# Attention features feeding a gated MLP on one core: the first batch alone, four MLP blocks instead of five beside the attention, the key sums on VectorE, gates after both halves

## The chip, the cores and the metric

The kernel runs on one core of a Trainium2 chip. The metric is the device time of one execution in microseconds; the median of three runs of the kernel before is 1408.88 us (1406.63 to 1411.75). TensorE (PE) multiplies matrices, VectorE (DVE), ScalarE (ACT) and GpSimd (POOL) work element by element, and SyncE (SP) issues all of the kernel's DMAs from one queue. Every engine takes its own instructions in the order in which they stand.

## The reference

```python
B, H, S, D, F = 8, 8, 576, 64, 128          # attention; the MLP is 4608 x 512 -> 1536 -> 512
def phi(x):
    proj = x @ w_phi                          # 64 -> 128
    proj = proj - max(abs(proj), axis=-1)
    return concat([exp(proj), exp(-proj)])    # 256 features
q_p, k_p = phi(q), phi(k)
kv = k_p.T @ v                                # per batch and head
z = sum(k_p, axis=tokens)
attn = (q_p @ kv) / (q_p @ z + 1e-6)
x = attn.reshape(4608, 512)
gate = 1 / (1 + exp(-(x @ w_gate)))
out = (gate * (x @ w_val)) @ w_out
```

All in float32. The MLP's weights come as float64 and are split on the chip into two float32r parts, `wh` and `wl`; x and the gated product are split alike (`xh`, `xl` and `hh`, `hl`), and each product of the MLP is three matmuls: high by high, and twice high by low.

## The kernel before

**Attention.** The 64 heads are 32 steps of two heads (a pair), four steps to a batch. A step projects the keys (`keys`, `rest`: tiles `pk`) and the queries (`q_half`: `pq`), takes the maximum of the keys on DVE, subtracts it (`dk`) and has ACT make the exponentials `ek` (`k_exp`); `q_max` does the maximum of the queries across partitions with a transposing reduction, small copies (line 506 has four of them) and a transpose, and subtracts it (`d`); `q_exp` makes `eq`. `kv` multiplies the key features by v into `kvz`, whose last third is the normalizer z; `turn` transposes it, `num` makes numerators `nm` and denominators `dp`; `norm` sends the denominators through two small DMAs (`dn`, `den`), takes the reciprocal, reads it back broadcast (`rb`) and multiplies (`xp`). x of batch 0 goes straight into `xh` and `xl` of the MLP's chunks 0 and 1; all of x goes to DRAM (`xscr`).

**MLP.** The hidden layer has 12 blocks of 128 (`j`). The first `JA` = 5 blocks run beside the attention (stage one), in 18 chunks of 256 tokens: a unit is one block of one chunk, two halves of 12 matmuls of 256 columns (gate, then value) into the two halves of one PSUM tile `gv`. The output of a chunk is two `acc` groups of three matmuls of 512 columns per block, stored to DRAM as y. After that, `rest_chunks` runs the other 7 blocks (stage two) in 9 chunks of 512 tokens, with matmuls of 512 columns (`g`, `v`, `acc2`), adds the stored y and writes the output. The weights of stage one are prepared by `weigh` between the first steps, three tiles to a block; those of stage two by `load_weights`, whose first pool takes the place of the attention's buffers, so that it runs while stage one ends.

**What sets the order.** In stage one the order on every engine is that of the program. A step has four places, each a call of `fill`: it adds to `due` and takes the halves and outputs whose turn has come from the list `ready`. Everything that follows a matmul (gate work, exponentials, sums, norm) is a generator in `tasks`: each `tick` advances all of them by one `yield`. `queue` puts the chunks of a finished batch in line `LAG` places later, `TILES` says how many weight tiles are granted by which step. Chunks that have no x yet are loaded by `load_x`.

In `half` the gate half is followed at once by ScalarE's two functions, which read the half that is done while the value half is still to be written to the same tile:

```python
            mm_in(gv[:, m, :], xs[c], js[i], m, CH)
            if m == 0:
                ...
                act.activation(t, gv[:, 0, :], AF.Tanh, scale=0.5)
                act.activation(u, gv[:, 0, :], AF.Exp)
            else:
                start(gate(c, i, n))
```

The normalizer's sum over the four 128-token tiles of keys is made by POOL (`k_sum`, lines 457 to 461) from step 4 on (`EARLY`); the steps before multiply each tile by ones on PE.

Of the kernel before, what the change touches and what calls it, by code (L numbers as in the profile page):

```python
# [33 lines left out]
JA = 5  # L34
JR = 8
EARLY = 4
DIRECT = 2
RATE = 3.0
LAG = (7, 9)
TILES = (1, 3, 5, 8, 11, 15)  # L40
# [4 lines left out]
def attention_moe(  # L45
# [154 lines left out]
    def half_units(js, mp, ps_gv, ps_acc):  # L200
        xs, hs, gvs, cs = {}, {}, {}, set()

        def load_x(c):
            xh, xl, raw = x_tiles(mp, CH, f"1_{c}")
            xs[c] = xh, xl
            nc.sync.dma_start(raw, xscr[c])
            for _ in range(3):
                yield
            act.copy(xh, raw)
            yield  # L210
            vec.tensor_tensor(xl, raw, xh.bitcast(F32), op=ALU.subtract)  # L211

# [4 lines left out]
        def gate(c, i, n):  # L217
            gv = gvs.pop((c, i))
            u, t, hh, hl = hs[c, i]
# [6 lines left out]
            vec.tensor_tensor(hl, u, hh.bitcast(F32), op=ALU.subtract)  # L226

        def half(c, i, m):
            if c not in xs:
                begin(c)  # L230
                for _ in range(4):
                    tick()
# [3 lines left out]
            gv = gvs[c, i]  # L236
            mm_in(gv[:, m, :], xs[c], js[i], m, CH)
            if m == 0:
                u = mp.tile([P, CH], F32, tag="u", name="u" + n)
                t = mp.tile([P, CH], F32, tag="t", name="t" + n)  # L240
                hh = mp.tile([P, CH], F32R, tag="hh", name="hh" + n, bufs=7)
                hl = mp.tile([P, CH], F32R, tag="hl", name="hl" + n, bufs=7)
                hs[c, i] = u, t, hh, hl
                act.activation(t, gv[:, 0, :], AF.Tanh, scale=0.5)  # L244
                act.activation(u, gv[:, 0, :], AF.Exp)  # L245
            else:
                start(gate(c, i, n))
                if i >= 1:
                    begin(c + 1)

        def half_out(c, t):
            acc = ps_acc.tile([P, DM], F32, tag="acc", name=f"acc1_{c}_{t}")
            for i, j in enumerate(js):
                mm_out(acc, t, (*hs[c, i][2:], None), j, i == 0, i == len(js) - 1)
            y = mp.tile([P, DM], F32, tag="y", name=f"y1_{c}_{t}")
            act.activation(y, acc, AF.Copy, scale=0.5)  # L256
            nc.sync.dma_start(yscr[c][t], y)

        def chunk(c):
# [3 lines left out]
            for i in range(len(js)):  # L263
                for m in range(2):
                    items.append((1.45, lambda i=i, m=m: half(c, i, m)))
                if i < 2 and c:
                    items += outs(c - 1)[i : i + 1]
            return items

# [3 lines left out]
        return chunk, outs, xs  # L273
# [60 lines left out]
    with ExitStack() as actx:  # L334
# [74 lines left out]
        def k_exp(i, gs, pps, ns):  # L409
# [14 lines left out]
            if i < DIRECT:  # L424
                for g, pp, mx, e in zip(gs, pps, mxs, es):
                    mn = at.tile([P, 4], F32, tag=f"mn{g}", name=f"mn{i}_{g}")
                    vec.tensor_scalar(mn[:, :ns], mx[:, :ns], -1.0, None, op0=ALU.mult)
                    for t in range(ns):
                        for sg in (1, 0):
                            act.activation(  # L430
                                e[:, t, sg * F : sg * F + F], pp[:, t, :], AF.Exp,
                                bias=(mn, mx)[sg][:, t : t + 1], scale=1.0 - 2.0 * sg,
                            )
                return
# [17 lines left out]
        def k_sum(i):  # L452

            es = ks[i]
            su = at.tile([P, 2, 2 * F], F32, tag="su", name=f"su{i}")
            for hd in range(2):
                pool.tensor_tensor(su[:, hd, :], es[hd][:, 0, :], es[hd][:, 1, :], op=ALU.add)  # L457
                for t in (2, 3):
                    pool.tensor_tensor(su[:, hd, :], su[:, hd, :], es[hd][:, t, :], op=ALU.add)
            for hd in range(2):  # L460
                pool.tensor_tensor(
                    su[head(hd), hd, :], su[head(hd), hd, :], es[2][head(hd), 0, :],
                    op=ALU.add,
                )
            es.append(su)
# [9 lines left out]
        def rest(i):  # L475
# [4 lines left out]
            def go():  # L480
                yield from k_exp(i, (2,), [pp], 1)
                if i >= EARLY:
                    yield
                    k_sum(i)
# [31 lines left out]
        def kv(i):  # L516
# [13 lines left out]
            for t in range(4, 5) if su else range(5):  # L530
                for o in range(0, P, Q):
                    hd, sg = divmod(o // Q, 2)
                    fs = slice(sg * F, sg * F + F)
                    if su:
                        a, x = ones, su[0][:, hd, fs]
                    else:
                        a = ones if t < 4 else halves[:, hd, :]
                        x = (e0, e1)[hd][:, t, fs] if t < 4 else e2[:, 0, fs]
                    nc.tensor.matmul(
                        kvz[o : o + Q, 2 * F :], a, x,  # L540
                        start=t == 0 or bool(su), stop=t == 4, tile_position=(0, o),
# [53 lines left out]
        def norm(i, ex, dr):  # L595
            b, p = steps[i]
            dn = at.tile([P, 9], F32, tag="dn", name=f"dn{i}")
            rb = at.tile([P, S], F32, tag="rb", name=f"rb{i}", bufs=1)
            nc.sync.dma_start(dn, dr.rearrange("(o r) c -> o r c", r=Q)[:, 0, :])
# [3 lines left out]
            vec.reciprocal(dn, dn)  # L603
            nc.sync.dma_start(dens[i].rearrange("h (r c) -> (h r) c", c=9), dn)
# [5 lines left out]
            for _ in range(4):  # L610
# [3 lines left out]
            for c in range(S // CH if b == 0 else 0):  # L614
# [4 lines left out]
                split(xs[c][0][:, ps], xs[c][1][:, ps], xp[:, c * CH : c * CH + CH])  # L619
            t = 0  # L620
# [169 lines left out]
```

## Time and profile before

| | us |
|---|---|
| median of 3 runs | 1408.88 |
| profiled execution, its own time | 1405.74 |
| its span, first to last instruction | 1403.8 |
| busy: PE / PE weight loads | 1253.2 / 984.3 |
| busy: DVE / ACT / POOL | 787.9 / 538.4 / 175.3 |
| mean granted clock of TensorE, share of full | 0.961 |

The busy time of PE counts matmuls that overlap as one stretch; it says when PE had something in hand, not that it ran at its peak. An engine's idle time is put down to what ended it last. The granted clock is the share of TensorE's full 2.4 GHz that it was given; 0.5 is 1.2 GHz.

### The profile page before, as it was taken

How to read it: one execution, taken by the hardware profiler on the slowest of the kernel's cores; microseconds unless marked ns; L12 is line 12 of the kernel's file. 1: busy time of each engine (PE TensorE's matmuls, PEld its weight loads, DVE VectorE, ACT ScalarE, POOL GpSimd, SP SyncE). 2: the span in 40 equal slices, each digit the busy share in tenths (PEclk: the TensorE clock that was granted, in tenths of full speed). 3: DMA queues.
4: the chain of work that ended last, by engine and by line, in shares of the span. 5: the costliest groups of instructions: out<-in, count | busy, mean ns of one | idle time of the engine just before them, and what ended most of it. 6: DMA issues, size and time to landing. Idle time of an engine off the chain costs nothing.

```text
span 1403.8 us, 22704 instructions
## 1 busy us (share of the span) xinstructions
PE 1253.2 (89%) x9096; PEld 984.3 (70%) x9096; DVE 787.9 (56%) x1527; ACT 538.4 (38%) x1133; POOL 175.3 (12%) x230
## 2 busy tenths in 40 slices
PE   6666897887987999989888788999999999999998
PEld 3433666665765777766666777888888888888887
DVE  6878877654754777766546833773424434244233
ACT  5543554544453555554453332331212222222121
POOL 0022332312221331323110000000000000000000
PEclk9867899998998999999999999999999999999999
DMA  5666333232232233232216510641201202112010
GB/s 198 206 220 203 104 105 99 81 96 90 62 98 82 63 117 104 84 119 76 71 60 196 188 38 16 215 139 37 91 30 61 83 8 91 30 60 90 0 61 30
DMA packets 81737, 133.42 MB, mean 95 GB/s; under 512 B 18656, under 2 KB 38240, under 8 KB 81632
## 3 DMA queue, kind: packets, MB, share of 16 engines
q1 hardware_dynamic: 81632, 131.98, 29.3%
q8 instruction: 71, 1.16, 0.3%
q14 instruction: 34, 0.28, 0.1%
HBM read 93.91 MB, written 28.46 MB: 87 GB/s over the span
## 4 chain that ended last, share of the span: by engine, by line
PE 73%; DVE 10%; ACT 9%; DMA 5%; issue 2%; SPq 1%; DVEq 0%; ACTq 0%
PE acc L171 21%; PE gv L164 15%; PE g L164 12%; PE v L164 12%; PE kvz L524 4%; PE nm L575 3%; ACT ek L447 2%; PE dp L584 2%; ACT t L244 2%; DMA rb<-den 1%; PE pk L403 1%; ACT u L245 1%; ACT eq L561 1%; PE pq L393 1%; DMA den<-dn 1%
## 5 line engine op out<-in xcount | busy, mean ns | idle before, releaser
L164 PE MATMUL gv<-xh,wh 128*128 128x256 f32 x720 | 222.5, 309 | 84.4 <-ACT u L245 66.9
L164 PEld LDWEIGHTS gv<-xh,wh 128*128 128x128 f32 x720 | 141.9, 197 | 115.5 <-ACT u L245 84.2
L164 PE MATMUL gv<-xl,wh 128*128 128x256 f32 x720 | 208.9, 290 | 2.0 <-DVE xl L211 2.0
L164 PE MATMUL gv<-xh,wl 128*128 128x256 f32 x720 | 208.2, 289 | 0.0
L171 PE MATMUL acc<-wh,hh 128*128 128x512 f32 x432 | 172.9, 400 | 0.7 <-ACT y L256 0.7
L171 PE MATMUL acc<-wl,hh 128*128 128x512 f32 x432 | 170.0, 393 | 0.0
L171 PE MATMUL acc<-wh,hl 128*128 128x512 f32 x432 | 169.1, 391 | 0.0
L164 PEld LDWEIGHTS gv<-xl,wh 128*128 128x128 f32 x720 | 142.6, 198 | 3.4 <-DVE xl L211 2.9
L164 PEld LDWEIGHTS gv<-xh,wl 128*128 128x128 f32 x720 | 142.5, 198 | 0.0
L62 ACT CAST hh<-u 128x512 fp32r<-128x512 f32 x63 | 39.1, 621 | 201.1 <-DVE u L185 201.1
L224 ACT CAST hh<-u 128x256 fp32r<-128x256 f32 x90 | 36.5, 406 | 197.8 <-DVE u L223 197.6
L457 POOL TENSOR_TENSOR su<-ek 128x256 f32<-128x256 f32 x56 | 45.1, 806 | 510.0 <-issue 298.2
L183 DVE TENSOR_SCALAR t<-t 128x512 uint32<-128x512 uint32 x63 | 26.8, 426 | 138.6 <-ACT t L180 138.4
L524 PE MATMUL kvz<-ek,v 128*32 128x256 f32 x1280 | 87.7, 426 | 15.9 <-issue 8.7
L164 PE MATMUL g<-xh,wh 128*128 128x512 f32 x252 | 99.0, 393 | 0.0
L171 PEld LDWEIGHTS acc<-wh,hh 128*128 128x128 f32 x432 | 81.9, 190 | 24.1 <-issue 6.3
L164 PE MATMUL v<-xh,wh 128*128 128x512 f32 x252 | 98.6, 391 | 0.0
L164 PE MATMUL g<-xh,wl 128*128 128x512 f32 x252 | 98.5, 391 | 0.0
L164 PE MATMUL g<-xl,wh 128*128 128x512 f32 x252 | 98.5, 391 | 0.0
L164 PE MATMUL v<-xl,wh 128*128 128x512 f32 x252 | 98.4, 390 | 0.0
L164 PE MATMUL v<-xh,wl 128*128 128x512 f32 x252 | 98.2, 390 | 0.0
L180 ACT ACTIVATE t<-g 128x512 f32<-128x512 f32 x63 | 37.6, 597 | 150.8 <-PE g L164 150.7
(94 smaller groups left out, 2305.4 us busy)
## 6 DMA issues: line engine op xcount, KB each, us to landing
wraw<-w_moe SPq DMA_DIRECT2D x36, 512.0 KB
xl<-xs SPq DMA_DIRECT2D x34, 512.0 KB
k<-k SPq DMA_DIRECT2D x32, 320.0 KB
v<-v SPq DMA_DIRECT2D x32, 320.0 KB
q<-q SPq DMA_DIRECT2D x32, 288.0 KB
wh<-wtop SPq DMA_DIRECT2D x36, 256.0 KB
rb<-den SPq DMA_DIRECT2D x64, 144.0 KB
ys<-y SPq DMA_DIRECT2D x36, 256.0 KB
```

The source lines that it names most:

```text
L62: a = act.copy(h, x)
L164: nc.tensor.matmul(o, a[:, ws], x[:, cs], start=i == 0, stop=i == 11)
L171: nc.tensor.matmul(acc, a[:, ts], w[:, ws], start=first and i == 0, stop=last and i == 2)
L180: act.activation(t, g, AF.Tanh, scale=0.5)
L183: vec.tensor_scalar(tu, tu, 0x7FFFFFFF, None, op0=ALU.bitwise_and)
L224: act.copy(hh, u)
L244: act.activation(t, gv[:, 0, :], AF.Tanh, scale=0.5)
L447: act.activation(e[:, :, sg * F : sg * F + F], dk, AF.Exp, scale=1.0 - 2.0 * sg)
L457: pool.tensor_tensor(su[:, hd, :], es[hd][:, 0, :], es[hd][:, 1, :], op=ALU.add)
L524: nc.tensor.matmul(kvz[o : o + Q, : 2 * F], vx[:, 2 * t + hd, o % D : o % D + Q], (e0, e1)[hd][:, t, :] if t < 4 else e2[:, 0, :], start=t ...
L575: nc.tensor.matmul(nms[hf][o : o + Q, :], w[:, sg, o : o + Q], es[sg][:, o // D, cs], start=sg == 0, stop=sg == 1, tile_position=(0, o),)
L584: nc.tensor.matmul(dp[o : o + Q, :], w[:, 2, z : z + Q], es[sg][:, hd, hf * HS : hf * HS + HS], start=sg == 0, stop=sg == 1, tile_position ...
```

## The change

- Stage one has four blocks (`JA` = 4) and stage two eight.
- The first four steps (batch 0) run by themselves in a loop of their own, each step's `kv`, `turn` and `num` in one go; no MLP work stands beside them. Then `first()` puts chunks 0 and 1 in line block by block (a weight block serves both chunks before the next is needed); `need` grants and waits for a weight tile where a half asks for it. `RATE` and `LAG` are smaller, and `DIRECT` and `TILES` go.
- `k_sum` runs on DVE: per head one addition of 128x512 and one of 128x256; the last, half-filled tile of keys is left to PE, with `halves`.
- In `gate`, ScalarE's functions come after both halves, and the gate's work is spread over more ticks; `hh` and `hl` have 10 buffers instead of 7.
- A few DMA issues (`y`, `dn`, `den`, `xscr`) come a tick later, and `xp` one tick sooner after `rb`.

```diff
-JA = 5
+JA = 4
-EARLY = 4
-DIRECT = 2
-RATE = 3.0
-LAG = (7, 9)
-TILES = (1, 3, 5, 8, 11, 15)
+EARLY = NP
+RATE = 2.8
+LAG = (2, 8)
         def gate(c, i, n):
             gv = gvs.pop((c, i))
-            u, t, hh, hl = hs[c, i]
+            u = mp.tile([P, CH], F32, tag="u", name="u" + n)
+            t = mp.tile([P, CH], F32, tag="t", name="t" + n)
+            hh = mp.tile([P, CH], F32R, tag="hh", name="hh" + n, bufs=10)
+            hl = mp.tile([P, CH], F32R, tag="hl", name="hl" + n, bufs=10)
+            hs[c, i] = hh, hl, None
+            act.activation(t, gv[:, 0, :], AF.Tanh, scale=0.5)
+            act.activation(u, gv[:, 0, :], AF.Exp)
+            yield
             tu = t.bitcast(U32)
...
+            yield
             act.copy(hh, u)
             yield
             vec.tensor_tensor(hl, u, hh.bitcast(F32), op=ALU.subtract)
         def k_sum(i):
             es = ks[i]
+            s2 = at.tile([P, 2, 2 * F], F32, tag="s2", name=f"s2_{i}", bufs=1)
             su = at.tile([P, 2, 2 * F], F32, tag="su", name=f"su{i}")
+            es.append(su)
             for hd in range(2):
-                pool.tensor_tensor(su[:, hd, :], es[hd][:, 0, :], es[hd][:, 1, :], op=ALU.add)
-                for t in (2, 3):
-                    pool.tensor_tensor(su[:, hd, :], su[:, hd, :], es[hd][:, t, :], op=ALU.add)
...
+                e = es[hd]
+                vec.tensor_tensor(s2, e[:, 0:2, :], e[:, 2:4, :], op=ALU.add)
+                vec.tensor_tensor(su[:, hd, :], s2[:, 0, :], s2[:, 1, :], op=ALU.add)
+                yield
         def norm(i, ex, dr):
...
+            yield
             nc.sync.dma_start(dn, dr.rearrange("(o r) c -> o r c", r=Q)[:, 0, :])
...
-            for _ in range(4):
+            for _ in range(3):
                 yield
             xp = at.tile([P, S], F32, tag="xp", name=f"xp{i}")
+        for i in range(EARLY):
+            more = i + 1 < EARLY
+            if more:
+                keys(i + 1)
+                copies(q_half(i + 1, 0))
+            start(q_exp(i))
+            tick()
+            tick()
+            kv(i)
+            tick()
+            if more:
+                copies(q_half(i + 1, 1))
+                rest(i + 1)
+                start(q_max(i + 1))
+            tick()
+            turn(i)
...
+            num(i)
+            tick()
+            tick()
+            grant((0, 1, 2, 6)[i])
+        queue(0)
+        def first():
+            cs.update((0, 1))
+            items = []
+            for i in range(len(js)):
+                items += unit(0, i) + unit(1, i)
+            return items + outs(0)
```

How the order moves, at three places. On PE, inside a unit of a chunk in the middle of stage one (the rows around the seam between the gate half and the value half; `waits` names what the row waits for); before:

```order
L164 MATMUL gv_2_1_2697<-xh_2_2559,wh_615 128x256
L164 MATMUL gv_2_1_2697<-xl_2_2560,wh_615 128x256
L164 MATMUL gv_2_1_2697<-xh_2_2559,wl_616 128x256
L164 MATMUL gv_2_1_2697<-xh_2_2559,wh_615 128x256 [waits Activation_49]
L164 MATMUL gv_2_1_2697<-xl_2_2560,wh_615 128x256
```

and now, where the value half follows without a wait:

```order
L163 MATMUL gv_3_1_3031<-xh_3_2586,wh_933 128x256
L163 MATMUL gv_3_1_3031<-xl_3_2587,wh_933 128x256
L163 MATMUL gv_3_1_3031<-xh_3_2586,wl_934 128x256
L163 MATMUL gv_3_1_3031<-xh_3_2586,wh_933 128x256
L163 MATMUL gv_3_1_3031<-xl_3_2587,wh_933 128x256
```

The wait for ScalarE at the seam is gone; ScalarE now reads the tile when PE has left it.

On PE, where the MLP begins (the first matmuls into `gv` of chunk 0, block 0); before, after the keys and half of the queries of step 7:

```order
L403 MATMUL pk_0_1407<-wk,k_3_1202 128x128
L403 MATMUL pk_1_1408<-wk,k_3_1202 128x128
L393 MATMUL pq_00_1424<-q_3_1200,wk 128x288 [waits DMAHW4_49,Activation_49]
L393 MATMUL pq_01_1425<-q_3_1200,wk 128x288 [waits Activation_49]
L164 MATMUL gv_0_0_1430<-xh_0_629,wh_287 128x256
```

and now, after the keys and queries of step 4 (`k_0_694` and `q_0_696` belong to the first pair of batch 1):

```order
L411 MATMUL pq_00_893<-q_0_696,wk 128x288 [waits DMAHW0_49,Activation_49]
L411 MATMUL pq_01_894<-q_0_696,wk 128x288 [waits Activation_49]
L411 MATMUL pq_10_922<-q_0_696,wk 128x288 [waits Activation_49]
L411 MATMUL pq_11_923<-q_0_696,wk 128x288 [waits Activation_49]
L482 MATMUL pk_2_928<-wk,k_0_694 128x128 [waits Activation_49]
L163 MATMUL gv_0_0_981<-xh_0_561,wh_597 128x256 [waits DMAHW1_49]
L163 MATMUL gv_0_0_981<-xl_0_562,wh_597 128x256
L163 MATMUL gv_0_0_981<-xh_0_561,wl_598 128x256
L163 MATMUL gv_0_0_981<-xh_0_561,wh_597 128x256
L163 MATMUL gv_0_0_981<-xl_0_562,wh_597 128x256 [waits DVE_49]
```

The MLP begins three steps sooner, and its first matmuls wait for the x of the last step of batch 0 themselves.

The sums of step 4's keys; before, on POOL by themselves:

```order
L457 TENSOR_TENSOR su_966<-ek_0_802 128x256
L459 TENSOR_TENSOR su_966<-su_966,ek_0_802 128x256 x2
L457 TENSOR_TENSOR su_966<-ek_1_805 128x256
L459 TENSOR_TENSOR su_966<-su_966,ek_1_805 128x256 x2
L461 TENSOR_TENSOR su_966<-su_966,ek_2_852 64x256 x2
```

and now on DVE, among the norm of step 3 (`xp`, `xl`), the query's subtraction (`d`) and weight tiles (`wtop`, `wmid`, `wl`):

```order
L618 TENSOR_TENSOR xp_970<-ex_832,rb_865 128x576
L62 TENSOR_TENSOR xl_0_562<-xp_970,xh_0_561 128x256
L62 TENSOR_TENSOR xl_1_566<-xp_970,xh_1_565 128x256
L467 TENSOR_TENSOR s_4_976<-ek_0_888 128x512
L468 TENSOR_TENSOR su_977<-s_4_976 128x256
L518 TENSOR_TENSOR d_892<-d_892,mb_945 128x1152
L136 SCALAR_TENSOR_TENSOR wtop_1_966<-wraw_1_915,wtop_1_966 128x512
L467 TENSOR_TENSOR s_4_976<-ek_1_891 128x512
L468 TENSOR_TENSOR su_977<-s_4_976 128x256
```

DVE has four more instructions in each of the steps 4 to 31, behind a wait for `rb` that stands ahead of them; POOL has none left.

## Rows read from the trace of the kernel before

**Rows 1.** By stage: its us; busy PE, PEld, DVE, ACT, POOL; clock, DMA share, GB/s.

```profile
0.00:133.20 133.20, 83.42 (x858) 48.48 (x858) 96.10 (x199) 64.36 (x152) 19.11 (x29) 0.79 0.63 208
133.20:743.30 610.10, 537.61 (x5256) 409.03 (x5256) 396.49 (x806) 301.53 (x678) 156.16 (x202) 0.96 0.29 90
743.30:880.60 137.30, 113.17 (x720) 101.13 (x719) 72.59 (x166) 43.55 (x96) 0.00 (x0) 0.98 0.34 112
880.60:1403.80 523.20, 518.98 (x2269) 425.66 (x2267) 222.77 (x358) 128.96 (x208) 0.00 (x0) 1.00 0.20 68
```

**Rows 2.** Chain of waits in stage two: start us, us, engine and tile.

```profile
902.57 2.75 PE g L164 x12
...
910.81 2.75 PE g L164 x12
```

**Rows 3.** PE's waits from 133.2 to 743.3: us in total, times, longest us.

```profile
PE gv L164 <- ACT u L245: 43.5, 42, 2.3
PE gv L164 <- ACT xh L209: 17.1, 3, 5.8
```

**Rows 4.** Timeline of PE at a unit's seam: start us, us, [idle before <- releaser].

```profile
294.40 0.39 PE L164 MATMUL gv<-xh,wh 128*128 128x256 f32 x1 [1.37 <-ACT u L245]
...
295.70 0.28 PE L164 MATMUL gv<-xl,wh 128*128 128x256 f32 x1
```

**Rows 5.** PE's waits from 743.3 to 880.6.

```profile
PE gv L164 <- ACT u L245: 23.4, 23, 2.4
```

**Rows 6.** DVE's waits from 60 to 135.

```profile
DVE xp L613 <- DMA rb<-den: 14.1, 3, 5.2
```

**Rows 7.** Chain of waits near the end of stage one.

```profile
824.26 3.43 PE acc L171 x15
```

**Rows 8.** Timeline of PE: the keys of step 2 and of step 6 begin.

```profile
29.36 1.16 PE L403 MATMUL pk<-wk,k 64*128 64x128 f32 x16
...
108.16 1.38 PE L403 MATMUL pk<-wk,k 64*128 64x128 f32 x16
```

**Rows 9.** Chain of waits in step 1's norm.

```profile
42.73 3.29 DMA dn<-dr
...
48.48 4.86 DMA rb<-den
```

**Rows 10.** DVE's groups by form: busy us, mean ns of one, idle before.

```profile
L63 DVE TENSOR_TENSOR hl<-u,hh 128x512 fp32r<-128x512 f32 x63 | 43.6, 692 | 34.2 <-ACT hh L62 33.6
...
L223 DVE SCALAR_TENSOR_TENSOR u<-u,t 128x256 f32<-128x256 f32 x90 | 41.0, 455 | 2.8
...
L226 DVE TENSOR_TENSOR hl<-u,hh 128x256 fp32r<-128x256 f32 x90 | 39.7, 441 | 18.4 <-ACT hh L224 18.4
L506 DVE COPY pn<-pm 32x36 f32<-32x36 f32 x128 | 39.1, 305 | 2.4
...
L222 DVE SCALAR_TENSOR_TENSOR t<-t,gv 128x256 f32<-128x256 f32 x90 | 37.9, 421 | 96.1 <-PE gv L164 89.4 <-ACT d L469 5.0 <-ACT wtop L81 0.2
L221 DVE TENSOR_SCALAR t<-t 128x256 uint32<-128x256 uint32 x90 | 27.8, 309 | 43.3 <-ACT t L244 43.2
...
L137 DVE SCALAR_TENSOR_TENSOR wtop<-wraw,wtop 128x512 uint32<-128x512 uint32 x15 | 11.4, 759 | 0.8 <-ACT wtop L134 0.8
```

**Rows 11.** Line 506 by itself: duration in ns, shortest, median and longest.

```profile
L506 DVE COPY pn<-pm x128: 170/176/756, 14.8 to 711.3; 32x36 f32<-32x36 f32 x128
```

**Rows 12.** DVE's waits from 133.2 to 743.3.

```profile
DVE t L222 <- PE gv L164: 63.2, 48, 5.0
```

**Rows 13.** Three short stretches, two with the same 48 PE instructions (columns as Rows 1).

```profile
22.98:27.17 4.19, 4.19 (x48) 2.06 (x52) 1.69 (x3) 3.12 (x12) 0.00 (x0) 0.55 0.90 304
33.99:36.36 2.37, 2.37 (x48) 1.78 (x52) 2.30 (x4) 2.37 (x6) 0.00 (x0) 1.00 0.04 10
334.00:338.00 4.00, 3.29 (x13) 3.00 (x14) 1.23 (x1) 0.00 (x0) 0.00 (x0) 0.50 0.51 156
```

**Rows 14.** Timeline of PE where the first of these stretches begins.

```profile
22.98 4.19 PE L524 MATMUL kvz<-ek,v 128*32 128x256 f32 x40 [5.94 <-ACT ek L430]
```

More of the change, by code (lines that the diff above doesn't have):

```diff
@@ L226, in gate @@
             vec.tensor_tensor(hl, u, hh.bitcast(F32), op=ALU.subtract)
+            parts["h", c] += 1
         def half(c, i, m):
-            if c not in xs:
-                begin(c)
-                for _ in range(4):
-                    tick()
+            begin(c)
+            while parts[c] < NP:
+                tick()
+            need(js[i], m)
             n = f"1_{c}_{js[i]}"
@@ L235, in half @@
                 gvs[c, i] = ps_gv.tile([P, 2, CH], F32, tag="gv", name="gv" + n)
[L236 to L246, printed above, removed]
+            mm_in(gvs[c, i][:, m, :], xs[c], js[i], m, CH)
+            if m == 1:
                 start(gate(c, i, n))
@@ L251, in half_out, with store, unit @@
         def half_out(c, t):
+            need(js[-1], 2)
+            while parts["h", c] < len(js):
+                tick()
             acc = ps_acc.tile([P, DM], F32, tag="acc", name=f"acc1_{c}_{t}")
             for i, j in enumerate(js):
-                mm_out(acc, t, (*hs[c, i][2:], None), j, i == 0, i == len(js) - 1)
+                mm_out(acc, t, hs[c, i], j, i == 0, i == len(js) - 1)
             y = mp.tile([P, DM], F32, tag="y", name=f"y1_{c}_{t}")
             act.activation(y, acc, AF.Copy, scale=0.5)
-            nc.sync.dma_start(yscr[c][t], y)
+            def store():
+                yield
+                nc.sync.dma_start(yscr[c][t], y)
+            start(store())
+        def unit(c, i):
+            return [(1.45, lambda m=m: half(c, i, m)) for m in range(2)]
         def chunk(c):
@@ L263, in chunk @@
             for i in range(len(js)):
-                for m in range(2):
-                    items.append((1.45, lambda i=i, m=m: half(c, i, m)))
-                if i < 2 and c:
+                items += unit(c, i)
+                if i < 2:
                     items += outs(c - 1)[i : i + 1]
             return items
+        def first():
[4 more added lines that the diff above has]
+            return items + outs(0)
         def outs(c):
             return [(0.69 * len(js), lambda t=t: half_out(c, t)) for t in range(2)]
-        return chunk, outs, xs
+        return chunk, first, outs, xs, parts
     def rest_chunks(js, xp, mp, ps_gv, ps_acc, load):
@@ L529, in kv @@
                     )
-            for t in range(4, 5) if su else range(5):
+            for t in range(3, 5) if su else range(5):
                 for o in range(0, P, Q):
@@ L627, in norm, with need @@
                 t += w
-        chunk, outs, xs = half_units(list(range(JA)), moe, ps_gv, ps_acc)
+        weighed = []
+        def need(j, m):
+            while len(weighed) <= 3 * j + m:
+                grant(3 * j + m + 1)
+                tick()
+        chunk, first, outs, xs, parts = half_units(list(range(JA)), moe, ps_gv, ps_acc, need)
         ready, coming = [], []
-        cdone = wdone = spot = last = 0
+        cdone = wdone = spot = after = 0
         wq = []
@@ L646, in attention_moe, with fill @@
         due = 0.0
-        def fill():
-            nonlocal due, spot, last
+        def fill(n=TICKS):
+            nonlocal due, spot, after
             spot += 1
             while coming and coming[0][0] <= spot:
-                last, cs = coming.pop(0)
-                for c in cs:
-                    ready.extend(chunk(c))
-            left = (coming[0][0] if coming else last + 4 * NP + LAG[1] - LAG[0]) - spot
+                b, cs = coming.pop(0)[1:]
+                after = spot + 4 * NP + (0 if b else 6 + LAG[1] - LAG[0])
+                if b == 0:
+                    ready.extend(first())
+                else:
+                    for c in cs:
+                        ready.extend(chunk(c))
+            left = (coming[0][0] if coming else after) - spot
             due += min(RATE, sum(c for c, _ in ready) / max(1, left))
-            n = 0
             while ready and due >= ready[0][0] / 2:
@@ L662, in fill @@
                 due -= cost
-                n += 1
-            for _ in range(TICKS - n):
+                n -= 1
+            for _ in range(n):
                 tick()
@@ L708, in attention_moe @@
             fill()
-        for _, cs in coming:
+        for _, _, cs in coming:
             for c in cs:
```

100 lines of the change are left out of this document (55 added, 45 removed).

## The prediction

> **What bounds the kernel now.** I read the busy time by stage first [rows 1]; it cuts the span into four parts that have different limits. In the last 523.2 us (stage two) PE has work all the time at a granted clock of 1.00, so it is bound by PE: 7 blocks by 9 chunks, each a gate, a value and an output group. From one gate group to the next of its kind are 8.24 us [rows 2], and 63 times that is 519 us, so nothing is lost there. In the first 133.2 us seven steps of attention run without the MLP. PE has work for only 83 us at a clock of 0.79, DVE for 96; POOL is nearly idle. DVE is the fullest engine, and what it stands still for is the broadcast of the reciprocal, 14.1 us over three steps in the stretch from 60 to 135 [rows 6]. In the middle, 610.1 us, PE has work for 538 and DVE for 396; PE's list of waits names ScalarE's second gate function for 43.5 us, 42 times, and the x of a chunk that was asked for too late for 17.1 us, 3 times [rows 3]. The timeline shows the first of them from close by: the value half of a unit stands 1.37 us while ScalarE reads the gate half, and then its matmuls follow each other every 0.12 us [rows 4]. In the end of stage one, 137.3 us without attention, the same wait comes 23 times in 23 units, 23.4 us [rows 5].
>
> **The change part by part.** The sum is made against the profiled execution (1405.74 us, 3.1 below the median).
>
> *Stage two* gets an eighth block: 9 times 8.24 is 74.2 us [rows 2], all on the path, as PE has no gap there: 523.2 becomes 597.4. Its weights come from the same two functions; four blocks instead of three must be ready when it begins, the rest has 8.24 us more time than now, so I add nothing.
>
> The block that moves saves in stage one 18 units of 24 matmuls at 0.12 us, 2.9 us a unit [rows 4], and 108 output matmuls at 0.229 (15 in 3.43 us [rows 7]). Its gate and value matmuls are 52 us there and 18 groups of 2.75, or 49.5, in stage two [rows 2]; so the move alone gives less than 3 us of matmul time. The Trainium skill (TensorE: Matmul & The Clock Gate, Back-to-back issue gap) puts one matmul at its columns over 2.4 GHz and 2.5 ns, which makes 47.2 us of the one and 46.6 of the other: by the page, an estimate, the move would give 0.6 us and the sum come out 2 us later. The gain has to come from waits and from order.
>
> *End of stage one.* The work left when the attention ends is 23 units and 11 outputs now, 18 and 10 by the changed program's order. An output is 3.43 us now and 12 matmuls, 2.75, later [rows 7]. Of 137.3 us, 11 outputs are 37.7 and the wait at the seam 23.4 [rows 5]; the rest is 3.3 us a unit. Without the wait: 18 times 3.3 and 10 times 2.75, 87 us. What hid there was DVE's preparation of stage two's weights; DVE's 72.6 us [rows 1] lose five units of gate work and gain three weight tiles, about 74 us, which is 85% of the new stretch. For that lost cover I add 8: 95 us.
>
> *Middle.* PE: the waits of the list sum to 72 us with the small ones, so 538 are work. 67 units at 2.9 and 25 outputs at 3.43 are 280; the rest, less some 6 us behind the three x waits, where the granted clock fell to half (0.50 in the four microseconds after one of them [rows 13]), is 10.0 us a step for the 25 steps. Later it holds steps 4 to 31 (27.8, since step 4's projections fall before it), 54 units and 26 outputs: 278 + 157 + 72, and 0.2 a step for the key tile that PE now sums itself, 513 us. Waits: the seam's goes, at most back to 35 (43.5 by 54 of 67). The chunks whose load is issued just ahead of their first matmul are 2, 4, 6, 11 and 13, five instead of three by the planner's places; at 5.7 us each [rows 3] and 2 of half clock, 38. DVE: two additions of 128x512 and two of 128x256 are 2.27 us a step, at 692 and 441 ns of the nearest additions with both inputs in SBUF [rows 10]. Now 396.5 us [rows 1] hold 67 gates at 1.63 (the four groups of 309, 421, 455 and 441 ns) and some 22 us of x and weights; 10.6 a step remains. POOL's silence gives some back: line 506's copy takes 176 ns in the median and 305 in the mean, 756 at the longest [rows 10, 11], and in the timeline the long ones stand beside POOL's additions. Four copies a step, 0.5 us, and a like amount from the other small ones that I don't count. So 12.4 a step by 27.8, 54 gates, 13 x and some 7 weight tiles (five instructions each, at most 759 ns): 345 + 88 + 17 + 22 = 472 us. Both engines are then nearly full. If PE waited for its x alone the middle would be 551; if DVE lost what it loses in its densest stretch, 14.1 of 75 us [rows 6], it would be 581. I take 570.
>
> *Beginning.* From the first keys to the first MLP matmul: four steps, then one norm. From step 2 to step 6 a step takes 19.7 us now [rows 8], with three to four weight tiles in most; later there are 1.5 a step. DVE's own work, 10.6 and 1.5 tiles of 3, is 15; a step's chain is more serial than now, since its exponentials, `kv` and `num` follow in one go, and I take 17. Bounds: 15 and 19.7. The norm's larger transfers are 3.3 and 4.9, with 2.4 us between them [rows 9]; with two multiplications, the split and the weight work queued on DVE ahead of `xp` I take 18. From the first keys at some 4 us on that is 94 us, 86 to 105. The DMAs issued a tick later and `xp` a tick sooner cost nothing when DVE is ahead, and are in the DVE bound when it isn't.
>
> Sum: 94 + 570 + 95 + 597 = 1356 us of span, 1358 with what lies around it, and **1361 against the median**; I say 1360.
>
> **The rivals.** *Nothing waits* (0.13): PE sets the middle with short x waits, 533, and the end has no lost cover, 87; 94 + 533 + 87 + 597 and the 5 us around it are 1316. For it: DVE runs back to back in its dense stretches (DMA waits are nearly all that it loses there [rows 6]). Against it: both engines would have to be over 85% full while each waits for the other.
>
> *The seam's wait moves to the bank* (0.08): the change does not do what it says. The tile is now held through both functions and two DVE instructions after the value half, and the second unit after it needs the bank. If DVE comes late, PE stands as long as at the seam now: 35 us in the middle, 18 in the end, 1413 us; half of it 1387. It decides where DVE reaches the gate more than about 1 us late, a unit's 2.9 less the 1.4 of the two functions [rows 4] and 0.7 of the two instructions [rows 10].
>
> *Slower: DVE's queue sets the step* (0.11). DVE has 17 us of work a step in the middle. Each step its queue stands at `xp` for the broadcast, 4.7 us a time when the work between is short [rows 6], with one tick less between them now; and at the gate for PE's value half, 63.2 us over 67 units now [rows 12], 1.8 a step. That makes 23.5 us a step, 653 in the middle, and 1444. It is slower than before from 22.2 us a step on. For it: the sums come on top, in front of everything else. Against it: a DVE that is late finds the value half done, so both waits seldom come together.
>
> *The first batch runs cold* (0.08). Alone, PE has gaps before most of its groups; after PE had stood 5.94 us [rows 14] the granted clock was 0.55, for the most part the lower level of 1.2 GHz, and one step later 1.00, the level of 2.4; the same 48 instructions took 4.19 and 2.37 us [rows 13]. At that ratio four steps of 10 us cost up to 30 more, 1390 us. The Trainium skill (TensorE: Matmul & The Clock Gate, Why this matters for your kernels) says to avoid gaps between bursts since the clock falls to half; the trace agrees. It is a rule against this change, as it makes such gaps on purpose.
>
> **How the numbers follow.** The forecast itself, 1330 to 1395, has 0.60. A measurement of this kernel can tell about 0.3%, 4 us, from no change. Faster are the forecast, nothing waits, the cold batch and half of the moved wait: 0.85. Within 0.3%: 0.03, from the moved wait between half and full. Slower: 0.12. The range 1308 to 1402 leaves out the slow rival and the full moved wait, and a little of the fast one.
>
> **What would show it.** Right: first MLP matmul at 86 to 105 us; no PE wait for ScalarE between the halves; attention over near 664 and stage two from about 759, 597 long without gaps; POOL idle; line 506 near 176 ns throughout; DVE over 75% busy in the middle. Wrong: a step of over 22 us with DVE waiting for `rb`; PE waiting for DVE's reading of `gv`; a gap ahead of stage two for weights.

## The result, and the profile after

| us | before | after |
|---|---|---|
| median of four runs each | 1408.50 (1406.63 to 1411.75) | 1374.33 (1370.79 to 1376.35) |
| span of the profiled execution | 1403.8 | 1373.9 |
| mean granted clock, share of full | 0.961 | 0.951 |

The ratio of after to before is 0.9752, with a 95% interval of 0.9723 to 0.9781: 34 us faster, 14 more than the 1360 forecast and inside its range. It is faster although the granted clock is lower, and this is where the analysis starts. The first view is again the busy time by stage, with the columns of [rows 1]:

```profile
0.00:91.30 91.30, 55.40 (x678) 34.46 (x678) 61.07 (x136) 43.26 (x92) 0.70 (x6) 0.83 0.50 168
91.30:677.60 586.30, 505.84 (x5284) 375.80 (x5283) 416.64 (x915) 303.26 (x673) 0.00 (x0) 0.92 0.34 109
677.60:776.90 99.30, 86.43 (x556) 78.38 (x553) 70.64 (x162) 37.67 (x82) 0.00 (x0) 0.95 0.51 171
776.90:1373.90 597.00, 592.74 (x2593) 486.38 (x2591) 245.54 (x394) 144.34 (x235) 0.00 (x0) 1.00 0.18 60
```

Stage one ends at 776.9 instead of 880.6, 103.7 us sooner, and stage two is 73.8 longer. In the middle (the second row) PE is idle for 80 of 586 us at a clock of 0.92; before it was idle for 72 of 610 at 0.96 [rows 1]. So the waits of PE in the middle must have changed their kind, not their amount. PE's list of waits for 91.3 to 677.6 (us in total, times, longest):

```profile
PE gv L163 <- DVE xl L210: 28.1, 6, 5.9
PE gv L163 <- ACT xh L208: 24.8, 5, 7.5
```

ScalarE's gate functions, the first row of [rows 3] with 43.5 us, are gone. In their place stand two rows for the same thing, the x of a chunk whose load was asked for too late: 24.8 us for its high part and 28.1 for its low part, 52.9 together, where [rows 3] has 17.1 and no row for the low part. The timeline shows one of the five loads (chunk 4):

```profile
289.27 0.43 SPq L205 DMA_DIRECT2D xl<-xs  x1
...
290.91 0.49 PE L482 MATMUL pk<-wk,k 128*128 128x128 f32 x2
...
294.14 1.38 DVE L500 TRANSPOSE_TENSOR_REDUCE pm<-d 128x36 f32<-128x1152 f32 x1
...
294.67 1.03 ACT L208 CAST xh<-xl 128x1024 fp32r<-128x1024 f32 x1
...
295.75 0.58 PE L163 MATMUL gv<-xh,wh 128*128 128x256 f32 x1 [4.35 <-ACT xh L208]
...
297.19 1.38 DVE L513 STREAM_TRANSPOSE mb<-pm 128x1152 f32<-128x1152 f32 x1
298.50 0.65 DVE L467 TENSOR_TENSOR s<-ek 128x512 f32<-128x512 f32 x1
299.18 0.42 DVE L468 TENSOR_TENSOR su<-s 128x256 f32<-128x256 f32 x1
299.52 1.35 DVE L518 TENSOR_TENSOR d<-d,mb 128x1152 f32<-128x1152 f32 x1
300.79 1.22 DVE L210 TENSOR_TENSOR xl<-xl,xh 128x1024 fp32r<-128x1024 f32 x1
...
302.06 0.58 PE L163 MATMUL gv<-xl,wh 128*128 128x256 f32 x1 [5.74 <-DVE xl L210]
...
304.58 0.41 PE L163 MATMUL gv<-xh,wh 128*128 128x256 f32 x1
304.79 0.41 PE L163 MATMUL gv<-xl,wh 128*128 128x256 f32 x1
...
306.37 1.93 PE L528 MATMUL kvz<-ek,v 128*32 128x256 f32 x32
```

ScalarE begins the high part 5.4 us after the load is issued. PE does one matmul and stands again: DVE, in its fixed order, works from 294.14 on at the maximum of a query (`pm` to `mb`), at a sum and at a subtraction (`d`) before it makes `xl` at 300.79. Then the matmuls follow each other every 0.21 us, at a granted clock of 0.50 (from 302.1 to 305.0), until they are back at 0.12. From 291.4, where PE's last work before ended, to 306.37 are 15 us for 24 matmuls that take 2.9 at the full clock: 12.1 us lost, 10.1 of them standing and 2 at half clock. Five such loads would be 60. The same place in the kernel before (its timeline):

```profile
327.25 1.14 PE L584 MATMUL dp<-eq,kv 128*32 128x288 f32 x16
327.42 1.36 DVE L514 TENSOR_TENSOR d<-d,mb 128x1152 f32<-128x1152 f32 x1
...
334.01 1.23 DVE L211 TENSOR_TENSOR xl<-xl,xh 128x1024 fp32r<-128x1024 f32 x1 [2.68 <-ACT xh L209]
...
334.03 0.58 PE L164 MATMUL gv<-xh,wh 128*128 128x256 f32 x1 [5.63 <-ACT xh L209]
...
335.29 0.58 PE L164 MATMUL gv<-xl,wh 128*128 128x256 f32 x1 [0.68 <-DVE xl L211]
...
341.06 0.28 PE L164 MATMUL gv<-xh,wl 128*128 128x256 f32 x1
```

There DVE had the subtraction `d` behind it, was waiting for ScalarE's copy and made the low part at once, so that PE stood only 0.68 us for it. The 24 matmuls and the stand ahead of them, from 328.4 to 341.3, still took 12.9 us; without 0.9 us of transposes and seam wait between the halves that is some 9 more than at full clock without a stand.

What differs is the place in the step. In the changed kernel PE's last work ahead of each of the five late loads is line 482, which stands directly before the start of the query's maximum (`q_max`), and in all five DVE makes that maximum before `xl`; in the kernel before it is line 584, one place later, and the maximum is done. The diff has the reason: the second number of `LAG` went from 9 to 8, so that the chunks of a later batch begin one of a step's four places sooner. The prediction has no term for it.

In the end of stage one the only wait of note is for DVE, which must read the gate tile before PE writes into its bank again (PE's waits, 677.6 to 776.9):

```profile
PE gv L163 <- DVE t L229: 10.1, 3, 3.9
```

Where the MLP begins, PE has done the first matmuls of chunk 0 at 73.3 and then stands 12 us for the last step's x; the timeline shows PE and DVE's multiplication that it hangs on:

```profile
73.27 0.56 PE L163 MATMUL gv<-xh,wh 128*128 128x256 f32 x1
...
86.35 0.76 DVE L618 TENSOR_TENSOR xp<-ex,rb 128x576 f32<-128x576 f32 x1 [1.40 <-DMA rb<-den]
...
87.60 0.58 PE L163 MATMUL gv<-xh,wh 128*128 128x256 f32 x1 [12.06 <-ACT xh L61]
```

Stage two has no gaps, and its period is that of [rows 2]; the chain of waits has 8.22 us from one gate group to the next of its kind:

```profile
906.00 2.76 PE g L163 x12
...
914.22 2.76 PE g L163 x12
```

### The profile page after: what moved, and what is told of

The parts are those of the page before. It is cut to its first block, busy times and chain, and to the rows that moved or that the text cites. A ratio compares the mean times of both kernels' runs of the same rounds, so it can differ in the third digit from the quotient of the medians.

```text
span 1373.9 us, 22434 instructions
## 1 busy us (share of the span) xinstructions
PE 1240.4 (90%) x9104; PEld 975.0 (71%) x9104; DVE 793.9 (58%) x1606; ACT 528.5 (38%) x1082; POOL 0.7 (0%) x6
## 4 chain that ended last, share of the span: by engine, by line
PE 70%; DVE 17%; DMA 7%; ACT 3%; issue 2%; SPq 1%; DVEq 0%
PE acc L170 19%; PE g L163 14%; PE v L163 14%; PE gv L163 10%; PE kvz L528 3%; PE nm L578 3%; DMA den<-dn 2%; DMA rb<-den 2%; PE dp L587 2%; DMA wraw<-w_moe 2%; DVE d L518 2%; PE pq L411 1%; DVE pm L500 1%; DVE mb L513 1%; PE pk L421 1%
## 5 line engine op out<-in xcount | busy, mean ns | idle before, releaser
L163 PE MATMUL gv<-xh,wh 128*128 128x256 f32 x576 | 178.3, 310 | 47.0 <-ACT xh L208 24.8
L163 PE MATMUL gv<-xl,wh 128*128 128x256 f32 x576 | 171.7, 298 | 28.1 <-DVE xl L210 28.1
L163 PE MATMUL gv<-xh,wl 128*128 128x256 f32 x576 | 170.9, 297 | 0.0
L163 PEld LDWEIGHTS gv<-xh,wh 128*128 128x128 f32 x576 | 117.8, 205 | 65.5 <-ACT xh L208 25.8
L163 PEld LDWEIGHTS gv<-xl,wh 128*128 128x128 f32 x576 | 118.0, 205 | 30.3 <-DVE xl L210 29.7
L163 PEld LDWEIGHTS gv<-xh,wl 128*128 128x128 f32 x576 | 118.2, 205 | 0.0
L163 PE MATMUL g<-xh,wh 128*128 128x512 f32 x288 | 113.0, 392 | 0.0
L183 DVE SCALAR_TENSOR_TENSOR t<-t,v 128x512 f32<-128x512 f32 x72 | 49.4, 686 | 96.5 <-PE v L163 96.5
L170 PEld LDWEIGHTS acc<-wh,hl 128*128 128x128 f32 x432 | 81.3, 188 | 21.0 <-DVE hl L234 2.5
L454 ACT ACTIVATE ek<-dk 128x512 f32<-128x512 f32 (+1 forms) x192 | 87.6, 519 | 19.6 <-DVE dk L445 18.8
```

The lines of the kernel that those rows point to most:

```text
L163: nc.tensor.matmul(o, a[:, ws], x[:, cs], start=i == 0, stop=i == 11)
L170: nc.tensor.matmul(acc, a[:, ts], w[:, ws], start=first and i == 0, stop=last and i == 2)
L183: vec.scalar_tensor_tensor(t, t, 1.0, vl, op0=ALU.add, op1=ALU.mult)
L454: act.activation(e[:, :, sg * F : sg * F + F], dk, AF.Exp, scale=1.0 - 2.0 * sg)
```

## The experiments

Two theories came out of this. Mine: the change wins some 50 us by the gate's functions and loses part of it again to late loads of x. The rivals: the gain comes from the moved block or the sums, and the late loads cost nothing because another wait would take their place. Each ratio below is to the kernel before, run beside it on the same chip (medians of 1408.4 to 1410.8); "us" against another experiment is the difference of medians, so up to 2.4 us of it can come from the different chips.

### ScalarE's functions between the halves again

The changed kernel, with only this part undone.

```diff
             mm_in(gvs[c, i][:, m, :], xs[c], js[i], m, CH)
+            if m == 0:
...
+                act.activation(t, gv[:, 0, :], AF.Tanh, scale=0.5)
+                act.activation(u, gv[:, 0, :], AF.Exp)
             if m == 1:
```

> The changed kernel with one part undone: ScalarE's two functions again stand between the gate half and the value half. My theory (PE sets the pace of most of stage one, so the wait at the seam was lost time): PE waits for ScalarE come back, about 1 us for each unit whose halves follow each other, some 35 us in the middle and 18 in the end, 1374 becomes 1415 to 1430. Rival (DVE or the late x sets the pace and the seam's wait is hidden anyway): under 10 us, 1374 to 1384.

Measured: 1422.46 us, ratio 1.0102 [1.0084, 1.0119], 48 us slower than the changed kernel. PE's waits over the whole run:

```profile
PE gv L163 <- ACT u L250: 52.1, 54, 3.8
PE gv L163 <- DVE xl L211: 28.1, 6, 5.9
```

The wait at the seam is back, 52.1 us over 54 units. Beside it the wait for the late low part is unchanged, the one for the high part falls from 24.8 to 18.1 us. By stages the beginning is 4, the middle 32 and the end 8 us longer. In the end the seam has 20.0 of the 52.1 us, but the 10.1 us for DVE's reading are gone there: in the end the changed kernel pays back at the bank about half of what this part gives. Without this part the change would have been slower than the kernel before.

### The gate's functions alone, on the kernel before

```diff
             u, t, hh, hl = hs[c, i]
+            act.activation(t, gv[:, 0, :], AF.Tanh, scale=0.5)
+            act.activation(u, gv[:, 0, :], AF.Exp)
             tu = t.bitcast(U32)
...
-                act.activation(t, gv[:, 0, :], AF.Tanh, scale=0.5)
-                act.activation(u, gv[:, 0, :], AF.Exp)
```

> The kernel before with one part of the change alone: ScalarE's two functions after both halves. In the first call the same part, undone in the changed kernel, cost 48 us. My theory (the seam's 67 us of PE waits are lost time in the kernel before too): 1345 to 1370. Rival (there another wait takes their place, since DVE stands right behind each gate and POOL slows it): over 1390.

Measured: 1331.03 us, 0.9439 [0.9413, 0.9466]: two moved lines give 80 us, more than the whole change. By stage:

```profile
136.00:695.00 559.00, 526.67 (x5255) 408.26 (x5255) 396.59 (x804) 298.37 (x675) 158.92 (x202) 0.97 0.33 98
695.00:809.30 114.30, 107.10 (x720) 98.81 (x720) 73.16 (x169) 43.45 (x98) 0.00 (x0) 0.99 0.42 136
```

The middle lost 51 us and the end 23, against waits of 43.5 [rows 3] and 23.4 [rows 5]. So all the rest of the change, as it stands, costs 43 us (1331.0 to 1374.3). The next runs look for the reason.

### x asked for earlier

The changed kernel, with the first chunk of each batch loaded three places before its turn; nothing else moves.

```diff
+LEAD = 3
...
+        def ask(c):
+            cs.add(c)
+            begin(c)
...
             spot += 1
+            if coming and coming[0][1] and coming[0][0] <= spot + LEAD:
+                ask(coming[0][2][0])
```

> The changed kernel with one thing more: the x of the first chunk of each batch from batch 1 on is asked for three places before its first half instead of at it. In the changed kernel five such chunks held PE for some 12.6 us each (4.3 us for ScalarE's copy, 5 to 6 us for DVE's subtraction, and matmuls at half clock). My theory: these 63 us are mostly lost time, 1374 becomes 1315 to 1335. Rival (DVE uses these stretches to catch up and would hold PE elsewhere): less than 20 us, over 1354.

Measured: 1312.01 us, 0.9316 [0.9295, 0.9337], 62 us faster than the changed kernel. By stage:

```profile
92.60:612.80 520.20, 492.40 (x5296) 367.46 (x5296) 414.27 (x915) 301.82 (x674) 0.00 (x0) 0.98 0.39 123
```

Both waits for the x of loaded chunks are off the list, the middle falls from 586 to 520 us, and the clock rises from 0.92 to 0.98. 62 us for five loads is 12.4 each, as the timeline had it. This settles what the late loads cost in the changed kernel.

### The same on the kernel before, and on the kernel before with the gate moved

The same two edits in the older code (the direct chunks left out). First on the kernel before:

> The kernel before with x asked for three places sooner where a batch's first chunk begins, and nothing else. It has three late loads, 5.6 us of standing each and some 2 to 4 us of half clock behind it. My theory: 17 to 30 us come back, 1380 to 1393. Rival (a late load is hidden by the wait at the seam that follows): under 8 us, over 1401.

Measured: 1403.08 us, 0.9953 [0.9937, 0.9969], a gain of 6.6 us. The seam's wait over the whole run grew from 66.9 us over 65 units to

```profile
PE gv L165 <- ACT u L246: 74.7, 67, 4.7
```

Then on top of the kernel before with the gate's functions moved:

> The kernel before with ScalarE's functions after both halves and the sooner x, five blocks, POOL's sums, the first batch in the common loop. Alone the first of them gave 80 us. If these two are the whole of it, 1298 to 1312, level with the changed kernel with sooner x (1312) although nothing else of the change is in it. If four blocks, DVE's sums and the rest are worth something once x is in time, 1315 or more.

Measured: 1323.41 us, 0.9402 [0.9379, 0.9426], 8 us faster than with the gate alone by the medians, 5 by the ratios, whose intervals overlap. PE's waits over the whole run, first of the gate alone, then with the early x:

```profile
PE gv L164 <- ACT xh L209: 18.8, 3, 7.3
...
PE pq L393 <- ACT d L469: 12.2, 9, 5.4
...
PE gv L164 <- DVE xl L211: 2.0, 3, 0.7
```

```profile
PE pq L398 <- ACT d L474: 24.6, 13, 5.2
```

20.8 us of waits for x go, and 12.4 come back at the queries' projection. So in the older order the rival holds: three late loads, with the low part made at once, cost little, as other waits mostly take their place. In the changed order there are five, PE stands 10.6 us for each instead of 6.9 (52.9 by 5, 20.8 by 3), and hardly anything takes their place: the row of `pq` has 16.5 us over the whole run of the changed kernel and 17.9 with the early x. With x in time on both sides, the rest of the change is worth 11 us (1323.4 against 1312.0), no longer a loss of 43.

### Four blocks alone, on the kernel before

```diff
-JA = 5
+JA = 4
...
-TILES = (1, 3, 5, 8, 11, 15)
+TILES = (1, 3, 5, 8, 11, 12)
```

> The kernel before with four blocks beside the attention instead of five, and nothing else. With four blocks the planner's list runs dry before five batches (chunks 2, 4, 6, 11 and 13) instead of three, each time with a late load of x. My theory (the block itself is worth a few us, the two more late loads cost 8 to 12 us each): 1415 to 1440, slower than before. Rival (fewer blocks beside the attention gain by themselves): under 1400.

Measured: 1416.55 us, 1.0046 [1.0029, 1.0062], 6 us slower. PE's waits over the whole run:

```profile
PE gv L164 <- ACT u L245: 61.9, 48, 5.2
PE gv L164 <- ACT xh L209: 28.6, 5, 5.9
```

With four blocks five loads are late instead of three, without anything else of the change. They do not bring the long wait for the low part (3.4 us in all here). It goes with the place where a chunk begins. Where the second number of `LAG` is 8, it is 28.1 us: in the changed kernel and with the seam's functions put back; and below 30.0 us with POOL's sums, 15.8 with five blocks and 23.8 with the first batch in the common loop. Where it is 9, it is 2.0 us (the kernel before, and the gate alone) and 3.4 here. So neither the gate's place nor the sums, the number of blocks or the lone first batch makes it. No run moves `LAG` alone.

### Five or three blocks in the changed kernel

`JA` = 5 instead of 4, with one buffer of `y` instead of two so that the memory holds it.

> The changed kernel with five blocks beside the attention again (JA = 5, the y tile has one buffer instead of two to make room). My theory (a block costs PE much the same in either stage, 74 us in stage two, 77 in stage one, so the number of blocks hardly matters by itself): 1370 to 1390. Rival (the lighter stage one is what gained): back by 20 us or more, over 1394; the same by the other sign if stage one has idle time to fill, under 1362.

Measured: 1344.4 us, 0.9545 [0.9526, 0.9565], 30 us faster than the changed kernel, which my theory had not expected. PE's waits over the whole run tell why:

```profile
PE gv L163 <- DVE xl L210: 15.8, 3, 5.8
PE gv L163 <- ACT xh L208: 15.2, 3, 6.6
```

Three late loads instead of five. Whether that is the whole reason, the early x shows; with it, five blocks:

> The changed kernel with x asked for three places sooner (1312 in the first call) and with five blocks instead of four (y with one buffer). Without the sooner x, five blocks were 30 us faster than four, and had three late loads instead of five. My theory (the number of blocks matters by the late loads alone): 1303 to 1322, as with four. Rival (stage one has idle time that a fifth block fills): 1275 to 1290.

Measured: 1323.44 us, 0.938 [0.9353, 0.9407]. Now five blocks are 11 us slower than four (1312.0), not 30 faster. And 1323.4 is also what the kernel before has with the gate moved and the early x (1323.41), which has five blocks too: with x in time and five blocks, the rest of the change (sums, lone first batch, weights on demand, ticks, one buffer of `y`) comes to nothing in sum, and the 11 us come with four blocks instead of five. And three blocks with the early x:

> The changed kernel with the sooner x and three blocks instead of four beside the attention; five blocks took 1323, four 1312. If PE sets the pace everywhere, a block costs the same in either stage and the trend only follows the end of stage one: 1300 to 1312. If DVE now sets the step (PE has 16 us of work a step left, DVE 16 as well), the middle no longer shrinks by the 57 us that PE loses, stage two still grows by 74: 1320 to 1350.

Measured: 1339.27 us, 0.9507 [0.9483, 0.953], 27 us slower than four. DVE's waits in its middle, 92.1 to 590:

```profile
DVE xp L623 <- DMA rb<-den: 68.1, 24, 6.2
```

With four blocks this row has 29.4 us, 16 times. With three, DVE has less MLP work beside a step and comes to `xp` before the broadcast is there, 24 times.

### The sums on POOL again

The changed kernel with the older `k_sum`.

```diff
-                vec.tensor_tensor(s2, e[:, 0:2, :], e[:, 2:4, :], op=ALU.add)
-                vec.tensor_tensor(su[:, hd, :], s2[:, 0, :], s2[:, 1, :], op=ALU.add)
...
+                pool.tensor_tensor(su[:, hd, :], es[hd][:, 0, :], es[hd][:, 1, :], op=ALU.add)
+                for t in (2, 3):
+                    pool.tensor_tensor(su[:, hd, :], su[:, hd, :], es[hd][:, t, :], op=ALU.add)
```

> The changed kernel with the key sums back on POOL as before. My theory: DVE's work falls by 2.3 us a step and its small copies take 305 ns again instead of 174, 1.0 to 1.3 us a step; PE sets the pace, so the time moves little, 1366 to 1382. Rival (DVE sets the step): DVE has about 1.2 us a step less, 30 us less in all, 1340 to 1350; second rival (what POOL does to DVE costs more than the sums): 1390 or more.

Measured: 1382.11 us, 0.9812 [0.9797, 0.9827], 8 us slower. DVE's groups by form in the middle (busy us, mean ns, idle before), first with the sums on POOL, then in the changed kernel:

```profile
L513 DVE COPY pn<-pm 32x36 f32<-32x36 f32 x108 | 33.0, 306 | 2.0
L234 DVE TENSOR_TENSOR hl<-u,hh 128x256 fp32r<-128x256 f32 x54 | 29.2, 541 | 16.2 <-ACT hh L232 16.0
...
L622 DVE TENSOR_TENSOR xp<-ex,rb 128x576 f32<-128x576 f32 x26 | 25.5, 981 | 33.5 <-DMA rb<-den 31.6 <-DMA k<-k 1.8
L229 DVE SCALAR_TENSOR_TENSOR t<-t,gv 128x256 f32<-128x256 f32 x54 | 22.7, 421 | 7.2
```

```profile
L467 DVE TENSOR_TENSOR s<-ek 128x512 f32<-128x512 f32 x55 | 36.9, 671 | 0.0
...
L468 DVE TENSOR_TENSOR su<-s 128x256 f32<-128x256 f32 x55 | 23.4, 425 | 1.9
...
L229 DVE SCALAR_TENSOR_TENSOR t<-t,gv 128x256 f32<-128x256 f32 x54 | 22.8, 422 | 7.2
L234 DVE TENSOR_TENSOR hl<-u,hh 128x256 fp32r<-128x256 f32 x54 | 22.5, 418 | 13.6 <-ACT hh L232 13.4
...
L618 DVE TENSOR_TENSOR xp<-ex,rb 128x576 f32<-128x576 f32 x26 | 19.7, 756 | 31.8 <-DMA rb<-den 27.8 <-issue 4.0
L510 DVE COPY pn<-pm 32x36 f32<-32x36 f32 x108 | 18.8, 174 | 2.0
```

DVE takes on 60.3 us of sums (36.9 and 23.4), and its busy time in the middle is 416.6 us against 415.3: POOL's silence pays for them almost to the last microsecond. The small copies of line 510 (513 with POOL's sums) fall from 306 to 174 ns, `hl`, which reads two tiles of SBUF, from 541 to 418, `xp` from 981 to 756; line 229, whose second input is in PSUM, stays at 422. The waits for a late low part are 30.0 us with the sums on POOL, 28.1 with them on DVE: the sums are not what makes `xl` late.

### The first batch in the common loop

The changed kernel with the steps of batch 0 in the loop of the others, as before (`LAG` = (7, 8), and `TILES`, as in the kernel of four blocks alone).

```diff
-LAG = (2, 8)
+LAG = (7, 8)
+TILES = (1, 3, 5, 8, 11, 12)
...
-        for i in range(EARLY):
...
-        queue(0)
-        for i in range(EARLY - 1, N + 1):
+        for i in range(-1, N + 1):
```

> The changed kernel with the first batch in the common loop again, as before: steps overlap by one, chunks 0 and 1 come seven places after the batch, weights are granted by the old table. My theory: the MLP begins some 40 us later but seven steps are then done instead of four; what the change gained is the MLP work done by 133 us, four units of 2.9 us, and the 12 us wait of its first half is gone: 1372 to 1395. Rival (running the batch alone is a main source of the gain): over 1400.

Measured: 1367.13 us, 0.9694 [0.9666, 0.9721], 7 us faster than the changed kernel, outside what I expected. In its first 136 us PE is busy for 92.9 us and DVE for 107.6, against 87.6 and 103.4 of the changed kernel in the same time: running the batch alone lets the MLP begin sooner, but both engines get less done in that time. The late loads of x are still five here. So both improvements together:

> The changed kernel with the sooner x and the first batch in the common loop. Singly the two gave 62 and 7 us. If they add up, 1300 to 1308; if the common loop's gain was only that its late loads came at better places, 1309 to 1318.

Measured: 1304.6 us, 0.926 [0.9236, 0.9284], the fastest of all: 105 us under the kernel before and 70 under the changed one. 62 and 7 add up. Its middle:

```profile
135.30:606.00 470.70, 457.43 (x4921) 345.82 (x4920) 367.47 (x813) 274.97 (x618) 0.00 (x0) 0.99 0.36 110
```

PE is busy for 97% of the middle.

## Why the prediction was right, and where its steps failed

The direction and the main cause hold. In the size, the late x was priced too low by 28 us and the rest of the middle too high by 12; the end came 4 us longer and the beginning 3 shorter, so the span is 18 us over the sum. The profiled execution of before lay 3.1 us below its median and that of after 1.4 above, which leaves 13 us to the 1361 of the sum and 14 to the 1360 forecast. So part of the closeness is luck: errors of 28 and 12 us took each other off.

- **The seam's wait**, 35 and 18 us, is the gain: 53 expected, 48 measured when it was put back, 32 of them in the middle and 8 in the end. On the kernel before it is worth 80 by the medians, 71 by the profiled executions, where its waits sum to 66.9.
- **The late x** is the step that failed. The count of five was right, the price was not: "at 5.7 us each and 2 of half clock, 38". The middle lost 66 us to it, the whole kernel 62, against the early x. The row of before that I took the 5.7 from measures a load whose low part follows at once; I did not look at what the new order puts ahead of line 210 on DVE, a second stand of 5.7 us in the timeline shown. The five loads have 10.6 us of standing each (52.9 by 5), not 5.7; the 2 of half clock were right in the load shown.
- **The rest of the middle** was forecast 570 less 38, 532; with x in time it is 520. PE's own work was put at 513 us, and with x in time PE is busy for 492.4. DVE's work was overestimated too: 472 us against 416.6. My sum gives back half a microsecond a step for POOL's silence (12.4 is 10.6 and 2.27 less 0.5), 14 us in all, and as much again was named and not counted; it was 59. `hl`, `xp` and others with two inputs in SBUF are slowed too, not the small copies alone.
- **The move of a block alone**, "less than 3 us" by matmul time, holds on the side that can be read by itself (stage two grew by 73.8 us, 74.2 forecast), but that is not what the number of blocks decides. It sets how much MLP work is there to stand beside a step, and how many loads come late: 6 us loss alone, 11 gain over five blocks with x in time, 27 loss when it goes down to three.
- **The beginning** was forecast 94 and is 91.3, where the keys of the next step begin. The terms (4, four times 17, and 18) make 90, not 94, and 82 to 101 for the bounds. The first MLP matmul comes at 73.3, sooner than any of these, but PE then stands until 87.6 for the last x. That its length was right says nothing of its worth: undone, it gains 7 us, which I did not have as a case of its own.
- **The end** was forecast 95 and is 99.3; the moved wait of the rival shows there, 10.1 us, three times, and not in the middle. The attention ends at 677.6 and stage two begins at 776.9, 14 and 18 us later than I wrote, mostly by the late x of the middle.
- **DVE's queue sets the step**, the slower rival, did not happen: DVE waits 27.8 us for `rb` in the middle, 71% of it is busy (I had said over 75). Its wait appears with three blocks beside the attention, 68 us, and there the kernel is still faster than before.
- **The cold first batch** did not either: its clock is 0.83, where the longer first stage of before had 0.79 [rows 1]; the cold stretches came in the middle, after the late loads.
- POOL's silence, line 506 (now 510) at 174 ns in the median and 179 at the longest, stage two without gaps and no wait between the halves came as said.

What stays open: why the moved gate alone gains a little more than its waits sum to; whether the start one place sooner is by itself enough to put the query's maximum ahead of `xl`, as the order in the code and the traces suggest; and what the weight tiles on demand and the DMA issues a tick later do, which are hidden in a sum near zero (the sums of the keys gain 8 us and the lone batch loses 7). None of these was tried apart.

## What to carry to other kernels

When a wait is priced from the trace of before, look in the new order at every instruction that the waiting engine's supplier has ahead of it: a late load cost some 9 us of PE before and 12 after, and there were five instead of three. A start moved by one place changes what stands ahead on every other engine. And price a late load by the whole episode (stand, second stand, slow matmuls), then ask whether another wait would fill its place: here the same edit was worth 7 us in one order and 62 in another. A large change that gains should still be taken apart: two moved lines gave 80 us, and the rest lost 43 until the loads were asked for earlier.

## What was unexpected of the hardware

POOL's additions cost DVE nearly as much time as DVE needs to make them itself: 60.3 us of sums on DVE against 59 us by which its other work got shorter. The Trainium skill (SBUF — State Buffer, Who interferes with whom) says that copies in certain modes and instructions with two inputs in SBUF contend with GpSimd for a shared port and that the later one is blocked. The groups above agree: the copies, `hl` and `xp` (981 ns against 756) got shorter, line 229 with one input in PSUM did not. The single instructions show it more sharply. With the sums on POOL, 15 of the 54 `hl` in the middle took 0.74 to 0.97 us, and each of them ran beside an addition on POOL, whose spans in a profile are rough; none of the 37 without one took over 0.43. The subtraction `d` has both inputs in SBUF too and stayed at 1.36 us: it never ran beside an addition. `xl` did so for most of its length once and was no slower, so being beside one is not always enough.

In the load shown, stands of PE of 4.35 and 5.74 us with one matmul between them were followed by a stretch at 0.50, the lower level of 1.2 GHz, before 1.00 came back: matmuls every 0.21 us instead of 0.12 (the two stretches, with the columns of [rows 1]).

```profile
302.10:305.00 2.90, 2.90 (x13) 2.90 (x14) 0.94 (x2) 0.00 (x0) 0.00 (x0) 0.50 0.00 0
305.20:306.30 1.10, 1.10 (x11) 1.03 (x9) 0.00 (x0) 0.00 (x0) 0.00 (x0) 1.00 0.00 0
```

A stand of 4.34 us alone did not always do it: at 553.88 the matmul behind one still ran at 1.00, and the clock was 0.50 only behind the second stand, of 5.93 us.
